# An order of its own for scores and DFT pairs in each of three stages, and a one-element ScalarE copy in each burst

## The chip, the cores and the metric

The kernel runs on one core of one Trainium2 chip, as one launch. The metric is the device time of that launch in microseconds. TensorE (PE) multiplies matrices; VectorE (DVE), ScalarE (ACT) and GpSimd (POOL) do the elementwise work; SyncE (SP) issues most DMAs. PEld is PE's weight load, which a trace lists apart from the matmul.

## The reference

Two branches read the same 2048 x 640 input, and a sigmoid gate mixes them.

```python
def _A_ref(x, wqkv, wo):                      # H = 32 heads, Dh = 20
    qkv = (x @ wqkv).reshape(B, S, 3, H, Dh).transpose(2, 0, 3, 1, 4)
    q, k, v = qkv[0], qkv[1], qkv[2]
    scores = jnp.einsum("bhqd,bhkd->bhqk", q, k) * (Dh ** -0.5)
    p = softmax(scores)
    o = jnp.einsum("bhqk,bhkd->bhqd", p, v)
    return o.transpose(0, 2, 1, 3).reshape(B, S, D) @ wo
def _B_ref(x, dft_seq_re, dft_seq_im, dft_hid_re, dft_hid_im):
    a = jnp.einsum("bsd,ed->bse", x, dft_hid_re)
    b = jnp.einsum("bsd,ed->bse", x, dft_hid_im)
    return jnp.einsum("ts,bse->bte", dft_seq_re, a) - jnp.einsum("ts,bse->bte", dft_seq_im, b)
g = sigmoid((x * gate_w).sum(-1, keepdims=True))
return g * _A_ref(x, wqkv, wo) + (1 - g) * _B_ref(x, ...)
```

The second branch is two matrix products with DFT matrices: along the 640 features ("hidden"), then along the 2048 positions ("sequence"). All is float32; where the kernel wants one pass of the array it splits a value into a rounded part and a rest and adds three products.

## The kernel before, in words

A first part (L543 to L632) projects q, k and v, stores them to DRAM and prepares the weights of the second branch. Then comes the main loop (L1117 to L1124), 256 **cycles**. In each cycle attention and the second branch are woven together, and PE's instructions are issued in exactly the order of a string of letters.

Attention is cut into 32 units: a pair of heads and one half of the queries. A head has 20 features, so a head's product needs under 64 rows of the array; of each pair one head lies on rows 0 to 63 and the other on rows 64 to 127. These are the two **halves** of the array, and a matmul on one half can run beside one on the other. The letters are:

- **e** (L1060 to L1091): one score matmul, 62 rows by 512 columns, into a PSUM bank (L1081), and ScalarE's exp of it into the tile p (L1087). Two e, one on each half, make one step `i`; a cycle has eight e, four steps. The first e of a step calls `begin(i)`, which sets `now[0] = i`, runs what was put off to that step (`at_step`), and takes a p tile, of which there are five.
- **m** (`s_mm`, L184 to L196): one score matmul for the row maxima of a unit 43 steps ahead (LEAD), into a PSUM bank (L194), and VectorE's max over it (L196). A cycle has eight m. When a unit's maxima are complete, `max_nm` and `turn_max` (L208, L226) turn them into two rows that later scores take in as extra rows.
- **F** (`fill`, L1005): as many steps of the second branch as the plan `goals` gives to this place. A step is a **DFT pair**: two matmuls of 64 rows by 320 columns, one on each half, into the PSUM tiles yp0 and yp1.
- **B** (`burst`, L1095): first up to two or three waiting `extras` (reading out yp, adding results), then the 8 products p times v of two key tiles (`av_step`, L720; each shows as two matmul records), which use all rows of the array. At the end of a unit, every eighth burst, ScalarE evicts av into o (L733).

Scores of both kinds take their banks from one ring of five (`bank`, L142). A score may start when the reader of the score five places earlier is done.

The string is `ORDER` for nearly all cycles, and `LATE` from cycle 246, when no m are left. `FIRST` says, for each of the four steps of a cycle and for each kind, on which half the first of the two scores goes.

The second branch runs through three stages in the cycles. **Hidden** (cycles 0 to 55, 15 pairs a cycle): `hid_pair`, L489 to L533, matmul at L511, read out by ScalarE and VectorE at L520 and L521. **Sequence** (56 to 223, 16 pairs a cycle, three cycles to an output tile): `dft_step`, L784 to L832, matmul at L807, read out at L826 and L827. **Output** (224 on, 12 pairs a cycle): `out_tile`, L866 to L899, the output projection of tiles already normalised, matmul at L878, read out at L887 to L890. `goals` spreads a cycle's pairs evenly over the F of its string; ORDER has 15 F.

The read of a finished yp is put into `extras` with the due time `now[0]`, and follow-up work with `now[0] + 3` or the like; `run_extras` in a burst takes what is due.

Of the kernel before, what the change touches and what calls it, by code (L numbers as in the profile page):

```python
# [22 lines left out]
DH = 20  # L23
# [9 lines left out]

ORDER = "emFemFFFFemFeFFmeFFemFFFmmFFmeeB"
LATE = "eeeeFFFFFFeeeEB"
FIRST = {"e": (0, 0, 1, 1), "m": (1, 1, 1, 1)}


LEAD = 43
# [49 lines left out]
def mix_kernel(ctx: ExitStack, tc: tile.TileContext, xa, xh, wqk, wb, wr, cdft, wo, out):  # L91
# [83 lines left out]

    mx, nms, ends = {}, {}, []
    rows_, done_tiles = [], []
    now, later = [-1], {}

    def at_step(i, fn):  # L180
        later.setdefault(i, []).append(fn)
# [307 lines left out]
    def hid_pair(u):  # L489
        n, hf, k = u // 8, u // 4 % 2, u % 4  # L490
        _, _, factor, targets = FEATURE[n]
        ps = [new_y(z)[:, :HE] for z in range(2)]
        fresh = [(th, ri, hf, k) not in seen for _, th, ri in targets]
        seen.update((th, ri, hf, k) for _, th, ri in targets)
        rows = [a_scr[ri, hf, th, k] for _, th, ri in targets]
        olds = []
        for (_, th, ri), new, row in zip(targets, fresh, rows):
            old = None
            if th == ri:
                old = acc(ri, hf, k)  # L500
            elif not new:
                old = slots.pop(0)
                slots.append(old)
                at_step(now[0] + 4, functools.partial(sp.dma_start, old, row))
            olds.append(old)
        done_ = 0
        for d in range(ND):
            for a, b in ((0, 0), (0, 1), (1, 0)):
                for z in range(2):
                    r = slice(64 * z, 64 * z + 64)  # L510
                    pe.matmul(ps[z], lefts[n][a][r, d, k * P : k * P + P], rights[2 * n + hf][r, b, d],  # L511
                              start=done_ == 0, stop=done_ == 3 * ND - 1)
                done_ += 1
                if done_ < 3 * ND:
                    yield
        direct = [i for i, ((_, th, ri), new) in enumerate(zip(targets, fresh)) if new and th == ri]
        m = olds[direct[0]] if direct else raw_tile()[:, : 2 * HE].rearrange("p (s c) -> p s c", s=2)

        def read():
            act.activation(m[:, 0], ps[0], AF.Copy, scale=factor)  # L520
            dve.tensor_scalar(m[:, 1], ps[1], factor, 1.0, op0=ALU.mult, op1=ALU.mult)  # L521

        def add(sign, old):
            pool.tensor_tensor(old, old, m, op=ALU.add if sign > 0 else ALU.subtract)  # L524

        extras.append((now[0], read))
        ends_ = {(th, ri): i for i, f in enumerate(FEATURE) for _, th, ri in f[3]}
        for (sign, th, ri), new, row, old in zip(targets, fresh, rows, olds):
            if not new:
                extras.append((now[0] + 3, functools.partial(add, sign, old)))  # L530
            if th != ri or ends_[th, ri] == n:
                at_step(now[0] + (4 if new else 11), functools.partial(sp.dma_start, row, m if new else old))
        yield  # L533

    step = 0
# [248 lines left out]
    def dft_step(g):  # L784
        n, t, s = g // NS // HT, g // NS % HT, g % NS
        if s == 0:
            new_y(0), new_y(1)
            outs[n, t] = []
        if s % 8 == 0 and g // 8 + 3 < 2 * UNITS:
            cfin.append(load_c(g // 8 + 3))  # L790
        if s % 8 == 4 and cfin and 2 < g // 8 + 2 < 2 * UNITS:
            cfin.pop(0)()
        if s == 8:
            for _, th, hf in PRODUCTS[n][2]:
                tt = th * HT + t
                y = None
                if (tt, hf) in signs:
                    y = apool[0].tile([P, HE], F32, name="yt", bufs=4)
                    sp.dma_start(y, y_scr[tt, :, hf * HE : (hf + 1) * HE])
                outs[n, t].append(y)  # L800
        c = cparts[g // 8]
        cs = slice((s % 8) * P, (s % 8 + 1) * P)
        a = at[n % 2, s]
        for z, (cz, az) in enumerate(((0, 0), (0, 1), (1, 0))):
            for h in range(2):
                r = slice(64 * h, 64 * h + 64)
                pe.matmul(yp[h][:, :HE], c[r, cz, cs], a[r, az], start=s == 0 and z == 0, stop=s == NS - 1 and z == 2)  # L807
            if z < 2:
                yield
        w = g % (HT * NS) - 16  # L810
        if n + 1 == len(PRODUCTS) and w >= 0:
            d, r = divmod(w, 8)
            if r == 0 and d < ND:
                wos[d] = raw_tile()[:, :D]
                sp.dma_start(wos[d], wo[:, d])
            if r == 5 and d < ND:
                raw = wos.pop(d)
                for h in range(2):
                    wos[d, h] = a_tile(1, 2 * d + h)
                    split(wos[d, h][:, 0], wos[d, h][:, 1], raw[:, h * HE : (h + 1) * HE], pool, pool)  # L820
        if s == NS - 1:
            m = apool[0].tile([P, HE], F32, name="m", bufs=3)
            y0, y1 = yp[0][:, :HE], yp[1][:, :HE]

            def read():
                act.activation(m, y0, AF.Copy)  # L826
                dve.tensor_tensor(m, y1, m, op=ALU.add)  # L827

            extras.append((now[0], read))
            for out_, y in zip(PRODUCTS[n][2], outs.pop((n, t))):  # L830
                extras.append((now[0] + 5, functools.partial(finish_y, out_, t, m, y)))
        yield  # L832


# [31 lines left out]
    def out_tile(tt, hf):  # L866
        new_y(0), new_y(1)
        if hf == 0:
            k = tt - PRE[0]
            yo[tt] = f32(a_tile(1, 12 + k) if k < 4 else a_tile(0, k)).rearrange("p z c -> p (z c)")  # L870
            assert all(st[tt, h] == 0 for h in range(2))
            sp.dma_start(yo[tt], y_scr[tt])
        o = opre[tt]
        for d in range(ND - 1):
            for z, (oz, wz) in enumerate(((0, 0), (0, 1), (1, 0))):
                for h in range(2):
                    r = slice(64 * h, 64 * h + 64)
                    pe.matmul(yp[h][:, :HE], o[r, oz, d], wos[d, hf][r, wz], start=d == 0 and z == 0, stop=d == ND - 2 and z == 2)  # L878
                if (d, z) != (ND - 2, 2):
                    yield  # L880
        m = apool[0].tile([P, HE], F32, name="m", bufs=3)
        y0, y1 = yp[0][:, :HE], yp[1][:, :HE]
        g = gate[:, tt : tt + 1]

        def read():
            if now[0] < total - LEAD:
                act.activation(m, y0, AF.Copy, scale=g)  # L887
            else:
                dve.tensor_scalar(m, y0, g, 1.0, op0=ALU.mult, op1=ALU.mult)
            dve.scalar_tensor_tensor(m, y1, g, m, op0=ALU.mult, op1=ALU.add)  # L890

        def add():
            y = yo[tt][:, hf * HE : (hf + 1) * HE]
            pool.tensor_scalar(y, y, ngate[:, tt : tt + 1], float(signs[tt, hf]), op0=ALU.mult, op1=ALU.mult)
            pool.tensor_tensor(y, y, m, op=ALU.add)  # L895

        extras.append((now[0], read))
        extras.append((now[0] + 3, add))
        yield  # L899

    def finish_y(target, t, m, y):
# [84 lines left out]
        at_tile += n  # L986
    assert cycles[-1][1] <= last + 1
    late = -(-(total - LEAD) // 4)
    at_goal = 0
    for c0, c1, count in cycles:  # L990
        for c in range(c0, c1):
            share = count * (c + 1 - c0) // (c1 - c0) - count * (c - c0) // (c1 - c0)
            places = (LATE if c >= late else ORDER).count("F")
            goals[c] = [at_goal + share * (f + 1) // places for f in range(places)]
            at_goal += share

# [58 lines left out]

    heads = {"e": 0, "m": 2 * LEAD}

    held = []

    def score(kind):  # L1060
        hold, kind = kind == "E", kind.lower()
# [1 line left out]
        heads[kind] += 1  # L1063
        i, z = divmod(x, 2)
        h = z
        if kind == "m" or i <= 4 * late:
            h ^= FIRST[kind][(i - (LEAD if kind == "m" else 0) - 1) % 4]
        if kind == "m":
            s_mm(i, h)()
            if z:  # L1070
# [4 lines left out]
        if i < total:  # L1075
# [8 lines left out]
            def exp():  # L1084
                if z == 0 and hold:
                    begin(i)
                act.activation(pts[n, kt, qc][:, h], pt, AF.Exp, scale=float(DH) ** -0.5)  # L1087
                if z:
                    end(i)

# [4 lines left out]
    def burst(c):  # L1095
# [8 lines left out]
                held.pop(0)()  # L1104
        turned[:] = ends
        ends.clear()
        if c == HID - 1:
            start_dft()

# [5 lines left out]
        else:  # L1115
            score(kind)
    for c in range(total // 4):  # L1117
        for kind in "e" * (c == late) + (LATE if c >= late else ORDER):
            if kind == "F":
                fill(c)  # L1120
            elif kind == "B":
                burst(c)
            else:
                score(kind)  # L1124
# [125 lines left out]
```

## Time and profile before

| what | value |
|---|---|
| median of 3 runs | 1848.58 us (1848.13 to 1849.0) |
| the profiled execution | 1848.44 us |
| its span, first to last instruction | 1846.7 us |
| mean granted TensorE clock | 1.000 |
| ACT, busy share of the span | 67% |
| POOL, busy share of the span | 71% |
| DVE, busy share of the span | 79% |
| DMA, mean | 189 GB/s |

PE is shown as busy for nearly the whole span, but its matmuls are pipelined, their ends are modelled, and two of them can run side by side. So busy time says little here. What can be read is when each matmul starts: the distance between two starts on the same half is what the first of them cost. The burst is a good mark in every cycle, since L726 occurs nowhere else; the distance from one burst's first matmul to the next is the length of a cycle. For DVE and ACT the number in brackets is the idle time ahead of a group and what ended it.

### The profile page before, as it was taken

The numbers are of one execution on the slowest core, as the hardware profiler recorded it, in microseconds if no ns is written. First come the engines' busy times: TensorE is split into PE (matmuls) and PEld (weight loads), VectorE is DVE, ScalarE is ACT, GpSimd is POOL, SyncE is SP. The second block draws the span as 40 slices with busy tenths as digits, with TensorE's granted clock in tenths as the row PEclk, the third lists the DMA queues.
The fourth block names the chain that finished last, engine by engine and source line by source line (L and its number), as shares of the span: only waits on it lengthen the run. The fifth ranks groups of instructions, "written<-read, shape, count | busy, mean of one in ns | idle before, by whom it ended". The sixth has DMA issues, their size and how long they took to land. (4 is left out here: it accounts for less than half of the span.)

```text
span 1846.7 us, 45912 instructions
## 1 busy us (share of the span) xinstructions
PE 1838.3 (100%) x17917; PEld 1339.6 (73%) x17917; DVE 1460.3 (79%) x2428; ACT 1237.2 (67%) x2378; POOL 1302.8 (71%) x1102
## 2 busy tenths in 40 slices
PE   9999999999999999999999999999999999999998
PEld 8988977676776776776777777677677777766666
DVE  4157489888888888888888888888888888889953
ACT  4233377777777777776676677677667767777785
POOL 1379735666678987556889899866889998724444
PEclk9999999999999999999999999999999999999999
DMA  7899884777666675536577687646486856442224
GB/s 237 191 316 357 310 219 133 225 222 236 205 218 212 197 218 146 142 108 171 182 221 240 162 252 192 198 127 182 148 224 186 233 165 204 137 115 65 64 56 156
DMA packets 196014, 349.63 MB, mean 189 GB/s; under 512 B 54240, under 2 KB 107616, under 8 KB 194004
## 3 DMA queue, kind: packets, MB, share of 16 engines
q1 hardware_dynamic: 194515, 341.45, 61.6%
q0 software_dynamic: 1280, 5.25, 1.4%
q8 instruction: 141, 2.31, 0.5%
q14 instruction: 78, 0.63, 0.1%
HBM read 257.79 MB, written 88.65 MB: 188 GB/s over the span
## 5 line engine op out<-in xcount | busy, mean ns | idle before, releaser
L196 DVE TENSOR_REDUCE mx<-ps 128x1 f32<-128x512 f32 x2048 | 1300.4, 686 | 205.4 <-PE ps L194 188.3
L1087 ACT ACTIVATE p<-ps 128x512 f32<-128x512 f32 x2048 | 1088.2, 598 | 421.6 <-PE ps L194 221.9
L194 PE MATMUL ps<-kst,qst 60*128 60x512 f32 x2048 | 777.0, 413 | 0.6 <-ACT p L372 0.5
L1081 PE MATMUL ps<-qst,kst 62*128 62x512 f32 x2048 | 694.5, 414 | 0.0
L807 PE MATMUL yp<-x,part 64*128 64x320 f32 x5376 | 644.9, 306 | 0.0
L807 PEld LDWEIGHTS yp<-x,part 64*128 64x128 f32 x5376 | 582.9, 186 | 7.2
L1081 PEld LDWEIGHTS ps<-qst,kst 62*128 62x128 f32 x2048 | 332.1, 184 | 222.8 <-DVE mx L196 129.8
L726 PE MATMUL av<-p,v 128*21 128x512 f32 x4096 | 492.5, 596 | 0.0
L194 PEld LDWEIGHTS ps<-kst,qst 60*128 60x128 f32 x2048 | 367.5, 184 | 12.4 <-ACT p L1087 1.0
L133 POOL TENSOR_TENSOR part<-raw,part 128x1024 fp32r<-128x1024 f32 (+3 forms) x134 | 297.0, 2216 | 10.2
L726 PEld LDWEIGHTS av<-p,v 128*21 128x21 f32 x4096 | 95.3, 100 | 207.1 <-issue 206.1
L132 POOL CAST part<-raw 128x1024 fp32r<-128x1024 f32 (+2 forms) x127 | 125.2, 986 | 134.2 <-PE yp L807 100.8
L672 POOL TENSOR_TENSOR raw<-raw,raw 128x1024 f32<-128x1024 f32 x78 | 187.3, 2401 | 34.0 <-DMA raw<-in_cdft 22.3
L511 PE MATMUL yp<-wb,x 64*128 64x320 f32 x1680 | 206.9, 307 | 0.0
L511 PEld LDWEIGHTS yp<-wb,x 64*128 64x128 f32 x1680 | 179.4, 186 | 3.3 <-DVE x L521 0.2
L524 POOL TENSOR_TENSOR x<-x,raw 128x640 f32<-128x640 f32 x40 | 62.6, 1564 | 44.1 <-DVE raw L521 40.6
L133 POOL TENSOR_TENSOR x<-araw,x 128x320 fp32r<-128x320 f32 x96 | 84.0, 875 | 7.7
L878 PE MATMUL yp<-x,part 64*128 64x320 f32 x720 | 87.1, 308 | 0.0
L895 POOL TENSOR_TENSOR x<-x,m 128x320 f32<-128x320 f32 x30 | 26.2, 874 | 79.2 <-DVE m L890 73.2
L878 PEld LDWEIGHTS yp<-x,part 64*128 64x128 f32 x720 | 75.9, 185 | 2.7
L701 POOL TENSOR_TENSOR araw<-araw 128x320 f32<-128x320 f32 x80 | 70.0, 876 | 3.2 <-DMA araw<-a_scr 1.4
L905 POOL TENSOR_TENSOR yt<-yt,m 128x320 f32<-128x320 f32 x64 | 55.4, 877 | 10.2 <-DVE m L827 10.2
(110 smaller groups left out, 1375.0 us busy)
## 6 DMA issues: line engine op xcount, KB each, us to landing
raw<-in_cdft SPq DMA_DIRECT2D x188, 512.0 KB
araw<-a_scr SPq DMA_DIRECT2D x176, 160.0 KB
qk_scr<-p SPq DMA_DIRECT2D x40, 512.0 KB
w_scr<-wb SPq DMA_DIRECT2D x36, 400.0 KB
kst<-qk_scr SPq DMA_DIRECT2D x90, 160.0 KB
qst<-qk_scr SPq DMA_DIRECT2D x90, 160.0 KB
wb<-w_scr SPq DMA_DIRECT2D x8, 1600.0 KB
part<-in_xh SPq DMA_DIRECT2D x10, 1024.0 KB
```

What stands on the lines that cost most here:

```text
L132: e1.tensor_copy(dst1, src)
L133: e2.tensor_tensor(dst2, src, f32(dst1), op=ALU.subtract)
L194: pe.matmul(ps, q[b : b + KROWS, qt * P : (qt + 1) * P], k[b : b + KROWS, kc * 512 : (kc + 1) * 512], start=True, stop=True)
L196: return lambda: dve.tensor_reduce(mx[n][:, h, qt, kc : kc + 1], ps, axis=AX.X, op=ALU.max)
L511: pe.matmul(ps[z], lefts[n][a][r, d, k * P : k * P + P], rights[2 * n + hf][r, b, d], start=done_ == 0, stop=done_ == 3 * ND - 1)
L672: pool.tensor_tensor(raws[0], raws[0], raws[1], op=ALU.add if PRODUCTS[n][0][1][0] > 0 else ALU.subtract)
L701: pool.tensor_tensor(raws[0], raws[0], raws[1], op=ALU.add if PRODUCTS[n][1][1][0] > 0 else ALU.subtract)
L726: pe.matmul(av[32 * j : 32 * j + DH + 1, :], v[:, kt, h * (DH + 1) : (h + 1) * (DH + 1)], pp[qc][:, h, :], start=kt == 0, stop=kt == NS - 1)
L807: pe.matmul(yp[h][:, :HE], c[r, cz, cs], a[r, az], start=s == 0 and z == 0, stop=s == NS - 1 and z == 2)
L878: pe.matmul(yp[h][:, :HE], o[r, oz, d], wos[d, hf][r, wz], start=d == 0 and z == 0, stop=d == ND - 2 and z == 2)
L1081: pe.matmul(pt, k[b : b + KROWS + 2, kt * P : (kt + 1) * P], q[b : b + KROWS + 2, qc * 512 : (qc + 1) * 512], start=True, stop=True)
L1087: act.activation(pts[n, kt, qc][:, h], pt, AF.Exp, scale=float(DH) ** -0.5)
```

## The change

The one string becomes four plans, each a string with its own FIRST. The plan is chosen by the cycle. The pair of numbers at the places of `e` and `m` is the half of a step's first score.

```diff
-ORDER = "emFemFFFFemFeFFmeFFemFFFmmFFmeeB"
-LATE = "eeeeFFFFFFeeeEB"
-FIRST = {"e": (0, 0, 1, 1), "m": (1, 1, 1, 1)}
+HIDDEN = "emeFFmeFFFmeFFFmeFFmeFeFFFmFemmB", {"e": (0, 0, 1, 1), "m": (1, 1, 0, 1)}
+SEQUENCE = "emeFmFFFFemFeFFmeFFemFFFmmFFFmeeB", {"e": (0, 0, 1, 1), "m": (1, 1, 1, 1)}
+OUTPUT = "emFeFmFemeFFmeFFmeFFmFmFeFmeB", {"e": (1, 0, 0, 1), "m": (0, 1, 1, 0)}
+LATE = "eeeeFFFFFFeeeEB", {"e": (0, 0, 0, 0), "m": (0, 0, 0, 0)}
...
-    now, later = [-1], {}
+    now, at_cycle, later = [-1], [0], {}
+
+    def ended():
+        return min(now[0], 4 * at_cycle[0] + 3)
...
-        extras.append((now[0], read))
+        extras.append((ended(), read))
...
+    def plan(c):
+        return LATE if c >= late else OUTPUT if c >= edge[-1] else SEQUENCE if c >= HID else HIDDEN
+
...
-            places = (LATE if c >= late else ORDER).count("F")
+            places = plan(c)[0].count("F")
...
-        if kind == "m" or i <= 4 * late:
-            h ^= FIRST[kind][(i - (LEAD if kind == "m" else 0) - 1) % 4]
+        h ^= plan(at_cycle[0])[1][kind][(i - (LEAD if kind == "m" else 0) - 1) % 4]
...
-                act.activation(pts[n, kt, qc][:, h], pt, AF.Exp, scale=float(DH) ** -0.5)
+                newest[:] = [pts[n, kt, qc][:, h]]
+                act.activation(newest[0], pt, AF.Exp, scale=float(DH) ** -0.5)
...
         turned[:] = ends
         ends.clear()
+        if 4 * c + 4 < total:
+            act.activation(seen_, newest[0][0:1, 0:1], AF.Copy)
...
     for c in range(total // 4):
-        for kind in "e" * (c == late) + (LATE if c >= late else ORDER):
+        at_cycle[0] = c
+        for kind in "e" * (c == late) + plan(c)[0]:
```

Every `now[0]` in a due time of a read-out or of its follow-up (in `hid_pair`, `dft_step` and `out_tile`) becomes `ended()`, which never goes past the third step of the cycle. `seen_` is a tile of one element. The copy reads one element of the p tile half that the newest exp wrote, so ScalarE waits for that exp and then writes `seen_`.

The number of F is now 15 in HIDDEN, 16 in SEQUENCE and 12 in OUTPUT, one for each pair of the cycle. Every string still has eight e and eight m, four of each on either half.

More of the change, by code (lines that the diff above doesn't have):

```diff
@@ L529, in hid_pair @@
             if not new:
-                extras.append((now[0] + 3, functools.partial(add, sign, old)))
+                extras.append((ended() + 3, functools.partial(add, sign, old)))
             if th != ri or ends_[th, ri] == n:
-                at_step(now[0] + (4 if new else 11), functools.partial(sp.dma_start, row, m if new else old))
+                at_step(ended() + (4 if new else 11), functools.partial(sp.dma_start, row, m if new else old))
         yield
@@ L827, in read @@
                 dve.tensor_tensor(m, y1, m, op=ALU.add)
-            extras.append((now[0], read))
+            extras.append((ended(), read))
             for out_, y in zip(PRODUCTS[n][2], outs.pop((n, t))):
-                extras.append((now[0] + 5, functools.partial(finish_y, out_, t, m, y)))
+                extras.append((ended() + 5, functools.partial(finish_y, out_, t, m, y)))
         yield
@@ L895, in add @@
             pool.tensor_tensor(y, y, m, op=ALU.add)
-        extras.append((now[0], read))
-        extras.append((now[0] + 3, add))
+        extras.append((ended(), read))
+        extras.append((ended() + 3, add))
         yield
@@ L1056, in mix_kernel @@
     heads = {"e": 0, "m": 2 * LEAD}
-    held = []
+    held, newest = [], []
+    seen_ = const.tile([1, 1], F32, name="seen")
     def score(kind):
```

## The prediction

> **What bounds the kernel now.** I read the page first, then single cycles of the trace, engine by engine, then windows by stage.
>
> ```profile
> span 1846.7 us, 45912 instructions
> ```
>
> The profiled execution took 1848.44 us, so 1.74 us lie around this span; the median of the runs, 1848.58, is 0.14 above it. To get at the stages I asked for the busy time of the max reductions (L196) in three windows that begin and end at bursts. Columns: window, its length, DVE busy time and count, clock, DMA.
>
> ```profile
> 240.99:578.98 337.99, 274.55 (x433) 1.00 0.68 205
> 585.39:1640.76 1055.37, 848.99 (x1337) 1.00 0.63 182
> 1647.34:1763.32 115.98, 94.47 (x152) 1.00 0.28 79
> ```
>
> A cycle has eight reductions, so these are 54, 167 and 19 cycles: 6.26 us a cycle in the hidden stage, 6.32 in the sequence stage, 6.10 in the output stage. The clock is full throughout. They hold 1509 of the 1847 us; nothing outside the cycles is touched. Now one sequence cycle, PE alone (start, length, group):
>
> ```profile
> 1002.33 0.63 PE L726 MATMUL av<-p,v 128*21 128x512 f32 x4
> ...
> 1004.66 0.39 PE L194 MATMUL ps<-kst,qst 60*128 60x512 f32 x1
> ...
> 1004.89 0.75 PE L807 MATMUL yp<-x,part 64*128 64x320 f32 x8
> ...
> 1008.26 0.42 PE L1081 MATMUL ps<-qst,kst 62*128 62x512 f32 x2
> 1008.62 1.91 PE L726 MATMUL av<-p,v 128*21 128x512 f32 x16
> 1010.46 0.49 PE L1081 MATMUL ps<-qst,kst 62*128 62x512 f32 x1
> ```
>
> From burst to burst 6.29; the burst holds PE from 1008.62 to 1010.46, 1.84 us. Between, each half of the array has its own stream. A score takes 0.235 us of its half (1004.66 to 1004.89), a fill 0.147 (eight fills are four a half: 0.75 less the 0.31 of the last, over three). A half has eight scores and 16 fills: 8 x 0.235 + 16 x 0.147 = 4.23. About 0.10 is lost when scores follow the burst, and 0.12 from the end of the last score to the burst (1008.26 to 1008.62 less 0.235). The sum is 4.23 + 0.22 + 1.84 = 6.29, what was measured. **The sequence stage is bound by the array itself**, with nothing left between. By the same sum the hidden stage (15 fills) should take 6.15 and the output stage (12) 5.71; they take 0.11 and 0.39 more. What ends last there:
>
> ```profile
> 403.89 0.63 PE L726 MATMUL av<-p,v 128*21 128x512 f32 x4
> 405.73 0.50 PE L1081 MATMUL ps<-qst,kst 62*128 62x512 f32 x1
> 406.31 5.15 DVE L196 TENSOR_REDUCE mx<-ps 128x1 f32<-128x512 f32 x8 [0.70 <-PE ps L194]
> 408.97 2.48 DVE L196 TENSOR_REDUCE mx<-ps 128x1 f32<-128x512 f32 x4
> 409.52 0.39 PE L194 MATMUL ps<-kst,qst 60*128 60x512 f32 x1
> 409.75 0.46 PE L1081 MATMUL ps<-qst,kst 62*128 62x512 f32 x2
> 410.14 1.05 PE L726 MATMUL av<-p,v 128*21 128x512 f32 x7
> ```
>
> Scores share five PSUM banks in turn, so a score waits for the reader of the score five places before it. In the old order e8 stands five behind m5. The fifth reduction starts at 408.97 (four are left from there), takes 0.69, ends at 409.66, and the two last e start at 409.75. **PE stood still for a bank.** The output stage shows the same more strongly:
>
> ```profile
> 1001.71 1.88 DVE L196 TENSOR_REDUCE mx<-ps 128x1 f32<-128x512 f32 x3
> 1702.29 0.63 PE L726 MATMUL av<-p,v 128*21 128x512 f32 x4
> 1704.71 5.00 DVE L196 TENSOR_REDUCE mx<-ps 128x1 f32<-128x512 f32 x8 [0.28 <-PE ps L194]
> 1707.91 0.55 PE L1081 MATMUL ps<-qst,kst 62*128 62x512 f32 x2
> 1708.40 1.92 PE L726 MATMUL av<-p,v 128*21 128x512 f32 x16
> 1709.98 0.55 DVE L890 SCALAR_TENSOR_TENSOR m<-yp,gate,m 128x320 f32<-128x320 f32 x1 [0.27 <-ACT m L887]
> ```
>
> Reductions back to back step by 0.60 (the row of three: 1.88 less 0.68, over two). Here the chain is a loop: burst, first m, five reductions on DVE, bank free, e8, burst. DVE idles only 0.28 and 0.27 in 6.1 us.
>
> **The change part by part.**
>
> *Order of the hidden stage.* The scores now stand e1 m1 e2 m2 e3 m3 e4 m4 e5 m5 e6 e7 m6 e8 m7 m8. e8 stands behind e5, and m5's bank is wanted by m7, with a score, four fills and another score (0.235 + 4 x 0.147 + 0.235 = 1.06) or more between on its half. I set the start of every score by its half's sum and asked for each bank's reader: m1's reduction begins 0.58 after the first score (405.73 to 406.31), the next ones 0.60 apart or 0.47 after their score. An exp begins 0.59 after the first score, or 0.47 after its own, takes 0.60, and PE starts some 0.1 after its end (as 409.66 to 409.75). The tightest are m3, at 0.10 + 2 x 0.235 + 5 x 0.147 = 1.31 on its half, with e1's exp over at 0.59 + 0.60 and the bank free at 1.29, and m8 (3.95, e6's bank free at 3.9). m7 wants m5's bank at 3.95; that reduction ends at 3.05 + 0.69, so it is free at 3.8. So none stops PE, barely, and the floor is 6.15. Both halves still carry 8 scores and 15 fills. The last reduction and the read of yp (L521) move later, to about 2.0 us after the burst's start; the first fill on the second half then stands at 2.4, so that is hidden too. Gain at most 0.11 a cycle, at least 0. I take 0.085, because two banks come free with hardly 0.05 to spare: 55 cycles x 0.085 = **4.7 us** (0 to 6.1).
>
> *Order of the output stage.* Scores: e1 m1 e2 m2 e3 m3 e4 m4 e5 m5 e6 m6 m7 e7 m8 e8. Now m8 stands five behind m5, and it is issued together with e8, so the loop stays. What goes is the gap in the five reductions (eight took 5.00; 7 x 0.60 + 0.69 is 4.89) and part of the wait for e8: m5 done at 1704.71 + 4 x 0.60 + 0.69 = 1707.80, pair at 1707.85, burst 0.39 to 0.43 later, at 1708.24 to 1708.28 against 1708.40. I take 0.10 for 21 cycles (the 22nd has no m left): **2.1 us** (0 to 3.4). DVE's wait for L887 goes as well, since ACT has one exp after the burst's start instead of two, but DVE then waits longer for m1: worth nothing.
>
> *Order of the sequence stage.* The old string has 15 fill places for 16 pairs, and the last place took two; the new one has 16. Beyond this only e2 moves ahead of the first fill. The halves' sums stay, m1's wait and the end stay: **0**. The bounds: 6.32 less 6.29 over 167 cycles, 5 us, is all that could go; nothing shows that it would.
>
> *The copy.* A ScalarE instruction of one element stands last in each burst, behind the exps, the read of yp and, where a head pair's unit ends, the eviction of av (L733).
>
> ```profile
> 89.14 0.16 ACT L396 ACTIVATE logit<-ps 128x1 f32<-128x1 f32 x1
> 89.18 0.45 ACT L392 ACTIVATE v<-ps 128x320 f32<-128x320 f32 x1
> 629.50 0.63 PE L726 MATMUL av<-p,v 128*21 128x512 f32 x4
> 631.53 0.60 ACT L733 ACTIVATE o<-av 128x512 f32<-128x512 f32 x1 [0.84 <-issue]
> 632.02 1.08 ACT L1087 ACTIVATE p<-ps 128x512 f32<-128x512 f32 x2
> 635.88 1.92 PE L726 MATMUL av<-p,v 128*21 128x512 f32 x16
> 1004.76 3.24 ACT L1087 ACTIVATE p<-ps 128x512 f32<-128x512 f32 x6 [1.24 <-PE ps L194]
> L1087 ACTq EVENT_SEMAPHORE  x403: 17/17/17, 587.8 to 1639.3; - x135
> ```
>
> In an ordinary cycle ACT waits 1.24 us ahead of its first exp: the copy lies in that gap and costs nothing, and its wait for the newest exp ends inside it too. Where a unit ends (every eighth burst) there is no gap: L733 cannot start before av is done, and e1's exp comes 0.49 behind it, 2.52 after the burst's start instead of 2.43 (1004.76 less 1002.33). That 0.09 already shows in full: this cycle takes 6.38. Behind the copy wait e1's exp, then m3 for its bank. The copy's price there has as ends 0.04 (89.14 to 89.18, the step from an activation of one column to the next) and about 0.28 (0.16 to 0.18 of its own and 0.10 of lost overlap). It may also save: the exps that reuse a p tile carry a semaphore instruction of 17 ns, which the copy may make needless, so the low end is -0.02. I take 0.05, nearest to the small activation's own row: 30 unit ends in these three stages x 0.05 = **+1.5 us** (-0.6 to +8.4).
>
> *The cap on due times* (ended): with e7 ahead of the last fills, now would be one step further; the cap puts due times where they were. 0.
>
> Sum: -4.7 - 2.1 + 0 + 1.5 = -5.3 on 1848.44, and 0.14 for the median: **1843.3 us**.
>
> **The rivals.**
>
> *A. The array keeps start order (slower).* The new orders put scores of one half in a row, so a half must run ahead. The trace shows how far it does so now:
>
> ```profile
> 1005.47 0.39 PE L1081 MATMUL ps<-qst,kst 62*128 62x512 f32 x1
> 1005.48 0.44 PE L194 MATMUL ps<-kst,qst 60*128 60x512 f32 x1
> 1005.71 0.45 PE L807 MATMUL yp<-x,part 64*128 64x320 f32 x3
> 1005.90 0.39 PE L1081 MATMUL ps<-qst,kst 62*128 62x512 f32 x1
> ```
>
> The program has one pair of fills between this m and the next e, but three fills start first: the third overtook an e that waited for its half. The old order needs one matmul overtaken, the new hidden and output orders two at one place each. If starts kept program order, a pair behind a score on the first half would leave the other idle: following the strings at 0.235 and 0.147 gives 0.65 more a hidden cycle, 0.09 a sequence cycle, 0.79 an output cycle, 36 + 15 + 17 = 68 us: 1917. It decides from the point where a second matmul has to be passed. The row of three speaks against it. The Trainium skill, TensorE: Matmul & The Clock Gate, "Part 3: Packing small matmuls — row/col tiling", says "MATMULs are pc-monotone in start AND end — strict FIFO, no reordering"; by that rule rival A holds, and the rows above disagree with it. Chance 0.08, and 0.03 for being slower in another way.
>
> *B. The gain does not come (within 0.2%).* Passing one matmul but not two costs 0.088 a hidden cycle (0.235 less 0.147), just what the bank gave: 1848. Or m3 and m8 find their banks late by some hundredths. Or the copy costs 0.28 at unit ends: 30 x 0.28 = 8.4, which with the 6.8 gained gives 1850.2. Together 0.33.
>
> *C. The copy removes no wait.* Should the exps keep the semaphore instruction of the row above, nothing changes in the sum: I have given it no gain. That case lies inside the forecast.
>
> **How the numbers follow.** Forecast 0.56, with both stages between half and all of their gain: 1838.5 to 1844.8. B 0.33, A and the rest 0.11. A measurement of this kernel tells about 0.2%, 3.7 us, from no change; so faster 0.56, same 0.33, slower 0.11. The range reaches from the full floors (-6.1 - 3.4 - 0.6 = -10.1) to B's upper end: 1838.5 to 1850.2.
>
> **What would show it.** Hidden cycles near 6.17 with the last two m less than 0.1 behind the fills; output cycles near 6.00 with eight reductions in about 4.9 us; sequence cycles at 6.29 still. Unit ends: the copy between L733 and e1's exp, and that cycle some 0.05 longer than 6.38. I am wrong if hidden cycles stay at 6.25 (banks or run-ahead), if sequence cycles move at all (then the array was not their bound), or if ACT's gap ahead of the first exp is gone in ordinary cycles.

## The result, and the profile after

| | before | changed |
|---|---|---|
| median of 4 runs each | 1848.37 us (1848.13 to 1849.0) | 1839.17 us (1838.49 to 1839.51) |
| profiled execution | 1848.44 us | 1838.49 us |
| ratio of the times | | 0.9948, 95% interval 0.9935 to 0.9961 |

The changed kernel is 9.2 us faster, 0.4 to 0.65%. In its code the lines have moved: a score e is L1089, its exp L1096, a score m L198, its max L200, the fills L515, L811 and L882, the burst's products L730, the eviction of av L737, and the copy is L1117.

The page of the changed kernel begins with its span; before it was 1846.7.

```profile
span 1836.7 us, 45512 instructions
```

It has 400 instructions fewer (45912 before), although a copy was added to 255 of the 256 cycles. That is the first thing to be explained. Next, the busy time of the max reductions in windows between the same bursts as before the change (columns: window, length, DVE busy and count, clock, DMA share, GB/s).

```profile
239.98:575.08 335.10, 274.40 (x433) 1.00 0.68 208
581.49:1632.72 1051.23, 846.09 (x1338) 1.00 0.62 183
1638.89:1753.32 114.43, 92.84 (x153) 1.00 0.29 80
```

The 54 hidden cycles fell from 337.99 to 335.10 us, the 167 of the sequence stage from 1055.37 to 1051.23, the 19 of the output stage from 115.98 to 114.43. Two of the prediction's windows end a little before the burst that they were to end at (at 578.98 and 1640.76, where the bursts start at 579.06 and 1641.03), so the whole cycles of before are 338.07 and 1055.64. **The largest gain, 4.4 us, lies in the sequence stage, for which the prediction had 0.** The rest of the difference in span, 10.0 less 8.9, is mostly the first burst, which starts 1.2 us earlier; it starts at 233.3 to 235.4 in the kernels below, whatever was edited, so nothing is read from it.

One hidden cycle, PE alone:

```profile
388.99 1.92 PE L730 MATMUL av<-p,v 128*21 128x512 f32 x16
390.84 0.50 PE L1089 MATMUL ps<-qst,kst 62*128 62x512 f32 x1
...
393.59 0.52 PE L1089 MATMUL ps<-qst,kst 62*128 62x512 f32 x2
...
394.56 0.40 PE L1089 MATMUL ps<-qst,kst 62*128 62x512 f32 x1
394.63 0.31 PE L515 MATMUL yp<-wb,x 64*128 64x320 f32 x1
394.78 0.40 PE L198 MATMUL ps<-kst,qst 60*128 60x512 f32 x2
395.11 0.63 PE L730 MATMUL av<-p,v 128*21 128x512 f32 x4
```

From burst to burst 6.12. The last e starts among the fills and no longer waits for m5's reduction; the last two m follow the last fill, and the burst follows them at 0.33. The floor in the prediction was 6.15. An output cycle, PE and then DVE:

```profile
1687.13 1.91 PE L730 MATMUL av<-p,v 128*21 128x512 f32 x16
...
1692.78 0.39 PE L198 MATMUL ps<-kst,qst 60*128 60x512 f32 x1
1692.78 0.39 PE L1089 MATMUL ps<-qst,kst 62*128 62x512 f32 x1
1693.10 0.63 PE L730 MATMUL av<-p,v 128*21 128x512 f32 x4
```

```profile
1688.43 0.55 DVE L894 SCALAR_TENSOR_TENSOR m<-yp,gate,m 128x320 f32<-128x320 f32 x1
1689.54 4.88 DVE L200 TENSOR_REDUCE mx<-ps 128x1 f32<-128x512 f32 x8 [0.56 <-PE ps L198]
```

5.97, with m8 and e8 side by side at the end, eight reductions in 4.88 (5.00 before), and DVE's wait moved from the read-out, which has none now, to the first m (0.56 instead of 0.28). All four points are those of the prediction. Now a sequence cycle, PE and then ACT:

```profile
996.85 1.92 PE L730 MATMUL av<-p,v 128*21 128x512 f32 x16
...
1000.01 0.39 PE L198 MATMUL ps<-kst,qst 60*128 60x512 f32 x1
...
1003.12 0.63 PE L730 MATMUL av<-p,v 128*21 128x512 f32 x4
```

```profile
998.08 0.20 ACT L1117 ACTIVATE seen<-p 1x1 f32<-1x1 f32 x1
999.23 3.27 ACT L1096 ACTIVATE p<-ps 128x512 f32<-128x512 f32 x6 [0.95 <-PE ps L198]
```

6.27 instead of 6.29. The copy lies in ACT's gap, as forecast. But two things differ from before. e1's exp starts 2.38 after the burst's start, not 2.43. And the third m (at 1000.01) takes 0.39, where the old one, at 1005.48 in the prediction's rows, took 0.44: it had found its bank late. What the copy takes away is counted in the view of the exp's own line, first before, then after (columns: durations in ns, first and last start; ACTq is ScalarE's sequencer):

```profile
L1087 ACTq EVENT_SEMAPHORE  x662: 17/17/38, 229.4 to 1818.7; - x166
```

```profile
L1096 ACTq EVENT_SEMAPHORE  x6: 17/17/254, 228.3 to 1770.3; - x6
```

656 semaphore instructions are gone and 255 copies came: 401 fewer, the 400 of the page but for one. (The new orders alone leave 613 of the 662, as x1_no_copy shows below; the copy alone leaves 6.) By the trace's records of sequence cycles before the change, e1's exp and the fifth exp of a cycle always, and the third in 43% of them, waited for two semaphores, PE's and ScalarE's own (an earlier exp had written the same p tile). Since the copy waits for the newest exp, later exps need only PE's.

### The profile page after: what moved, and what is told of

It is laid out like the page before. It is cut to its first block, busy times and chain, and to the rows that moved or that the text cites. A ratio compares the mean times of both kernels' runs of the same rounds, so it can differ in the third digit from the quotient of the medians.

```text
span 1836.7 us, 45512 instructions
## 1 busy us (share of the span) xinstructions
PE 1828.5 (100%) x17917; PEld 1327.4 (72%) x17917; DVE 1455.6 (79%) x2428; ACT 1261.9 (69%) x2633; POOL 1303.9 (71%) x1102
## 5 line engine op out<-in xcount | busy, mean ns | idle before, releaser
L200 DVE TENSOR_REDUCE mx<-ps 128x1 f32<-128x512 f32 x2048 | 1295.3, 685 | 208.0 <-PE ps L198 159.1
L1096 ACT ACTIVATE p<-ps 128x512 f32<-128x512 f32 x2048 | 1080.9, 599 | 379.8 <-PE ps L1089 195.5
L198 PE MATMUL ps<-kst,qst 60*128 60x512 f32 x2048 | 768.2, 409 | 1.2 <-DMA a_scr<-x 0.7
L1089 PE MATMUL ps<-qst,kst 62*128 62x512 f32 x2048 | 680.6, 406 | 0.0
L811 PE MATMUL yp<-x,part 64*128 64x320 f32 x5376 | 651.5, 306 | 0.0
L811 PEld LDWEIGHTS yp<-x,part 64*128 64x128 f32 x5376 | 590.0, 186 | 6.6
L730 PE MATMUL av<-p,v 128*21 128x512 f32 x4096 | 492.5, 596 | 0.0
L1089 PEld LDWEIGHTS ps<-qst,kst 62*128 62x128 f32 x2048 | 328.4, 184 | 221.8 <-DVE mx L200 123.9
L198 PEld LDWEIGHTS ps<-kst,qst 60*128 60x128 f32 x2048 | 360.6, 184 | 15.8 <-ACT p L1096 1.6
L730 PEld LDWEIGHTS av<-p,v 128*21 128x21 f32 x4096 | 95.3, 100 | 208.3 <-issue 207.0
L515 PE MATMUL yp<-wb,x 64*128 64x320 f32 x1680 | 212.5, 307 | 0.6 <-DVE x L525 0.6
L515 PEld LDWEIGHTS yp<-wb,x 64*128 64x128 f32 x1680 | 193.8, 186 | 5.0 <-DVE x L525 1.6
L882 PE MATMUL yp<-x,part 64*128 64x320 f32 x720 | 92.9, 311 | 0.0
L882 PEld LDWEIGHTS yp<-x,part 64*128 64x128 f32 x720 | 80.7, 186 | 1.8
```

Source lines behind the costliest of these rows:

```text
L198: pe.matmul(ps, q[b : b + KROWS, qt * P : (qt + 1) * P], k[b : b + KROWS, kc * 512 : (kc + 1) * 512], start=True, stop=True)
L200: return lambda: dve.tensor_reduce(mx[n][:, h, qt, kc : kc + 1], ps, axis=AX.X, op=ALU.max)
L730: pe.matmul(av[32 * j : 32 * j + DH + 1, :], v[:, kt, h * (DH + 1) : (h + 1) * (DH + 1)], pp[qc][:, h, :], start=kt == 0, stop=kt == NS - 1)
L1089: pe.matmul(pt, k[b : b + KROWS + 2, kt * P : (kt + 1) * P], q[b : b + KROWS + 2, qc * 512 : (qc + 1) * 512], start=True, stop=True)
L1096: act.activation(newest[0], pt, AF.Exp, scale=float(DH) ** -0.5)
```

## The experiments

Each kernel ran beside the kernel before the change, on the same chip. Cycle lengths are the median distance between the first matmuls of two bursts, in the profiled execution: ordinary cycles of each stage; hidden cycles whose burst holds `max_nm` (every eighth); sequence cycles whose burst ends a unit (every eighth). Over all sequence cycles that end no unit, the medians come out up to 0.01 higher. All in us.

| kernel | hidden | with max_nm | sequence | unit end | output |
|---|---|---|---|---|---|
| before | 6.24 | 6.25 | 6.288 | 6.38 | 6.10 |
| the change | 6.12 | 6.29 | 6.266 | 6.445 | 5.99 |
| x1_no_copy | 6.12 | 6.31 | 6.30 | 6.38 | 6.01 |
| x2_copy_alone | 6.20 | 6.21 | 6.265 | 6.44 | 6.06 |
| x13_copy_other | 6.12 | 6.32 | 6.285 | 6.46 | 6.00 |
| x3_sequence_alone | 6.24 | 6.24 | 6.293 | 6.37 | 6.085 |
| x5_hidden_alone | 6.12 | 6.30 | 6.30 | 6.37 | 6.085 |
| x6_output_alone | 6.24 | 6.24 | 6.30 | 6.38 | 6.01 |
| x4_copy_first | 6.12 | 6.28 | 6.266 | 6.38 | 5.99 |
| x10_unlevel | 6.24 | 6.325 | 6.266 | 6.45 | 5.99 |
| x8_gate_and_loads | 6.12 | 6.31 | 6.266 | 6.38 | 5.995 |
| x9_read_before_max | 6.125 | 6.17 | 6.266 | 6.37 | 5.99 |
| x11_ngate_on_pool | 6.13 | 6.17 | 6.266 | 6.38 | 5.99 |

**1. Orders or copy.** The change without the copy, the copy alone in the kernel before, and the change with a copy that reads another tile.

```diff
 # x1_no_copy, against the change
-        if 4 * c + 4 < total:
-            act.activation(seen_, newest[0][0:1, 0:1], AF.Copy)
 # x2_copy_alone, against the kernel before
+    held, newest = [], []
+    seen_ = const.tile([1, 1], F32, name="seen")
...
+                newest[:] = [pts[n, kt, qc][:, h]]
+                act.activation(newest[0], pt, AF.Exp, scale=float(DH) ** -0.5)
...
+        if 4 * c + 4 < total:
+            act.activation(seen_, newest[0][0:1, 0:1], AF.Copy)
 # x13_copy_other, against the change
+    still_ = const.tile([1, 1], F32, name="still")
+    dve.memset(still_, 0.0)
...
-            act.activation(seen_, newest[0][0:1, 0:1], AF.Copy)
+            act.activation(seen_, still_, AF.Copy)
```

> The change without the copy. My theory: the copy lets e1's exp start some 60 ns sooner in an ordinary cycle (0.53 instead of 0.59 us after the first score), and m3, which waits for e1's bank, is what the sequence cycle gains by. Then without it ordinary sequence cycles go back to about 6.29 us, unit-end cycles there go from 6.44 to about 6.38, and the time is about 1841 us (+3 and some tenths in the hidden stage, -1.4 and -0.6 at unit ends). Rival: moving e2 ahead of the first fill is the gain, and the copy only costs. Then ordinary sequence cycles stay at 6.265 and the time falls to about 1837 us.

> The kernel before with nothing but the copy. My theory: ordinary sequence cycles 6.265 instead of 6.29 (126 x 0.025 = -3 us), unit-end cycles there 6.44 instead of 6.38 (21 x 0.06 = +1.3), hidden and output stages unchanged since their bank waits are on VectorE: about 1846.7 us. Rival (the copy only costs): sequence cycles at 6.29, and 1849.5 to 1850 us.

> The changed kernel, with the copy of one element at the same place, but out of a tile of its own that is written once at the start, and not out of the newest p. It costs ScalarE the same and takes over no wait. Theory: the copy gains because it reads what the newest exp wrote, so that the next exp need not wait on its own engine's semaphore; without that, e1's exp begins 0.59 us after its score again (0.534 with the change), sequence cycles take 6.30 (6.265 with it), unit ends are still some 0.06 longer than with no copy, and the time is that of the change without the copy or a little more, 1844 to 1847. Rival: it gains because ScalarE has done something shortly before (any instruction would serve); then e1's exp begins at 0.53 to 0.54, sequence cycles take 6.265, and the time is near 1839 to 1840.

Measured: x1_no_copy 1845.31 (1842.57 to 1848.88), ratio 0.9979 [0.997, 0.9987]; x2_copy_alone 1843.58 (1842.06 to 1845.45), 0.9967 [0.9954, 0.998], both beside a before of 1849.01; x13_copy_other 1847.05 (1844.88 to 1848.73), 0.9984 [0.9975, 0.9993], beside 1849.22. So by the medians the three orders together gave 3.7 us and the copy alone 5.4: **more than half of the gain is the copy's**. The two add up to about the change (9.2, and 8.2 in part 6). x13_copy_other came out between its two theories: the time, 1847.05, is that of a copy that takes over no wait, e1's exp starts 0.534 after its score, as in the change, and the sequence cycle, 6.285, lies between. The lines of the exps show why, of x1_no_copy and of x13_copy_other:

```profile
L1096 ACTq EVENT_SEMAPHORE  x613: 17/17/38, 228.7 to 1817.3; - x154
```

```profile
L1098 ACTq EVENT_SEMAPHORE  x416: 17/17/38, 228.6 to 1818.6; - x139
```

By the records, this copy too waits for ScalarE's own semaphore, since it writes `seen_` again, and that wait is old enough to cover e1's exp and no more: of 147 sequence cycles that end no unit e1's exp has a second semaphore in none, the fifth exp still in all, the third in 63. With 613, 416 and 6 such instructions the sequence cycle is 6.30, 6.285 and 6.266. The own part of the wait is what counts, and a copy serves as far as its own wait reaches. Had any recent ScalarE instruction served, the fifth exp, with exps just ahead of it, would not have been late. It starts, after e1's score, at 2.754, 2.726 and 2.705 in the three kernels (medians). The third m, whose bank e1's exp frees, needs only e1's part: the next fill on its half follows it by 0.276, 0.238 and 0.232. What one wait costs is the step of e1's exp: 0.593 to 0.534, some 0.06 us, though the semaphore instruction is shown with 0.017.

**2. Each order alone**, without the copy: one new string, the old string in the other two stages.

```diff
 # x5_hidden_alone, against the change without the copy
-SEQUENCE = "emeFmFFFFemFeFFmeFFemFFFmmFFFmeeB", ...
-OUTPUT = "emFeFmFemeFFmeFFmeFFmFmFeFmeB", ...
+SEQUENCE = "emFemFFFFemFeFFmeFFemFFFmmFFmeeB", ...
+OUTPUT = "emFemFFFFemFeFFmeFFemFFFmmFFmeeB", ...
```

> The sequence stage's order alone, with no copy. My theory: sequence cycles at 6.29, time 1848.4 us as before. Rival (e2's move is the gain): sequence cycles at 6.265, time about 1844.5 us.

> The hidden stage's order alone, without the copy. My theory: ordinary hidden cycles fall from 6.24 to 6.12 us, but the order also brings three losses of its own: the gate's five small instructions (make_gate, due at step 40) now stand ahead of the cycle's last three reductions and cost cycle 10 about 1 us; after a unit's last maxima the read of yp ends too late for the next cycle's first fill, 6.30 instead of 6.25 in one cycle of eight; and the first reductions of unit 8 wait for a late load in cycle 53, 0 to 8 us from run to run. So about 41 x 0.12 = 4.9 gained, 1.0 + 0.4 + some 2 lost: 1847 us, between 1845 and 1851. Rival (the prediction's own working, nothing lost beside it): 1843.7 us.

> The kernel before with the OUTPUT order alone: no copy, the old order in the hidden and sequence stages. Theory: the loop through the five reductions and e8 gets 0.08 to 0.10 us shorter in each of 21 output cycles (6.09 to about 6.00), 1.7 to 2.1 us in all: near 1847 where before shows 1849. Rival: the output cycles gain only through the earlier first exp, which the copy gives; then they stay at 6.08 or more and the time is that of before within 0.5 us.

Measured: sequence alone 1847.86 (1847.31 to 1851.85), 0.9995 [0.9986, 1.0004] beside 1849.01; hidden alone 1845.66 (1844.25 to 1849.95), 0.9977 [0.9965, 0.9989] beside 1849.38; output alone 1847.28 (1845.83 to 1851.74), 0.9991 [0.9982, 1.0] beside 1849.22. The sequence order is worth nothing that can be measured. The output order takes some 0.08 from a cycle, and the sum of its 21 cycles goes from 128.39 to 126.87. The hidden order takes 0.12 from an ordinary cycle, more than the forecast's 0.085, and yet its 55 cycles sum to 340.89 instead of 344.29, 3.4 us and not 6.6. The table shows one leak: cycles whose burst holds `max_nm` are at 6.30. The other is a cycle of 7.5 us, the tenth. Both are followed up in part 5. Taken alone the three orders give 1.2 (within the noise), 3.7 and 1.9 us, 6.8 in all, and together (x1_no_copy) only 3.7. In the profiled executions cycle 53 is 4.0 too long in x1_no_copy and has no stall in x5_hidden_alone, which would account for the difference; it is not shown for the other executions.

**3. The copy's place.**

```diff
 # x4_copy_first, against the change
         run_extras(max(done - HIDS, 0) // 3, 3 if c <= HID else 2)
+        if 4 * c + 4 < total:
+            act.activation(seen_, newest[0][0:1, 0:1], AF.Copy)
         for kt in (2 * c, 2 * c + 1):
...
-        if 4 * c + 4 < total:
-            act.activation(seen_, newest[0][0:1, 0:1], AF.Copy)
```

> The change with the copy issued ahead of the burst's products, so that at a unit's end it stands before the eviction of av and not between that and e1's exp. My theory: the saving of the semaphore instruction stays in every cycle, and the cost at unit ends goes: e1's exp there at about 0.67 us after the first score instead of 0.77, unit-end sequence cycles at 6.36 instead of 6.44, hidden ones at 6.16 instead of 6.26; 21 x 0.08 + 7 x 0.1 = 2.4 less, about 1836.8 us. Rival (the eviction's own wait for av sets that cycle and the copy hides in it): no change, 1839.2 us.

Measured: 1838.23 (1836.49 to 1843.85), 0.9944 [0.9932, 0.9956] beside 1849.01. ScalarE at the end of a unit, in the change and in x4_copy_first:

```profile
1030.27 0.60 ACT L737 ACTIVATE o<-av 128x512 f32<-128x512 f32 x1 [0.51 <-POOL x L134]
1030.77 0.18 ACT L1117 ACTIVATE seen<-p 1x1 f32<-1x1 f32 x1
1030.86 3.15 ACT L1096 ACTIVATE p<-ps 128x512 f32<-128x512 f32 x6
```

```profile
1036.17 0.18 ACT L1109 ACTIVATE seen<-p 1x1 f32<-1x1 f32 x1
1036.81 0.60 ACT L737 ACTIVATE o<-av 128x512 f32<-128x512 f32 x1 [0.45 <-POOL x L133]
1037.30 3.17 ACT L1096 ACTIVATE p<-ps 128x512 f32<-128x512 f32 x6
```

In the change the exp starts 0.59 behind L737, in x4_copy_first 0.49: the copy puts 0.09 (1030.77 to 1030.86) into a chain without a gap. Moved ahead of the products it lies in a gap there too, the unit end falls from 6.445 to 6.38, and ordinary cycles keep 6.266.

**4. How far a half may run ahead.** All first m of a step on one half again, in the hidden stage: by the sum of its matmuls one half of the array would then run 0.47 ahead of the program's order, past three waiting matmuls.

```diff
-HIDDEN = "emeFFmeFFFmeFFFmeFFmeFeFFFmFemmB", {"e": (0, 0, 1, 1), "m": (1, 1, 0, 1)}
+HIDDEN = "emeFFmeFFFmeFFFmeFFmeFeFFFmFemmB", {"e": (0, 0, 1, 1), "m": (1, 1, 1, 1)}
```

> The change with the hidden stage's m on the halves that the other stages use, 1 1 1 1 instead of 1 1 0 1: the halves' sums stay equal, but from e5 to m6 one half must run 0.47 us ahead of the other instead of 0.235, passing three matmuls that wait instead of two. If PE takes any order across the halves: hidden cycles stay at 6.12 us, 1839 us. If a half can run ahead by no more than what the levelled order needs: 0.235 more a hidden cycle, 6.35 us, 13 us slower, 1852 us. By strict start order the levelled order itself could not have gained, so that is out already.

Measured: 1845.24 (1843.6 to 1847.83), 0.9972 [0.9961, 0.9984] beside 1849.38. Hidden cycles take 6.24 where the change takes 6.12. DVE and PE of x10_unlevel:

```profile
396.90 0.69 DVE L200 TENSOR_REDUCE mx<-ps 128x1 f32<-128x512 f32 x1
```

```profile
397.65 0.50 PE L1089 MATMUL ps<-qst,kst 62*128 62x512 f32 x1
...
397.99 0.45 PE L515 MATMUL yp<-wb,x 64*128 64x320 f32 x3
```

Behind this sixth e the next fill of its half starts 0.34 later, where 0.235 is the rule: 0.10 of the 0.12 are lost here. But the trace points to a bank, not to a limit on running ahead. The sixth e takes the bank of m3, the score five places before it, and m3's reduction is the DVE row above; it ends at 397.60. In 52 of 53 hidden cycles (all but the tenth) this e starts 0.054 to 0.057 behind the end of that reduction, early or late, and is shown with 0.49 to 0.50. In the change, where it stands behind m5 on its half, it starts 0.27 behind that end and is shown with 0.39. The e8 of the old output stage, which waited for its bank, has the same two figures, 0.054 and 0.50 (medians). The sixth e did overtake m5, which the program issues before it and which starts at 397.87. By this reading the new place of m5 brings the sixth e to a bank that is not yet free; no edit tests it. How many waiting matmuls a half can pass, no run here shows. That the halves are kept level is a part of the change that carries weight: 0.12 a cycle.

**5. The leaks of the hidden stage.** Three edits, one on top of the other, all with the copy placed first as in part 3. x8: `make_gate` moves from step 40 into the burst of the tenth cycle, behind the read-out, and two loads of rows that the hidden stage has written to a_scr (`load_a_early`) are issued one cycle later, clear of the loads of the next unit's scores. x9: the read-out goes ahead of `max_nm` in the burst. x11: the last product of the gate goes to POOL.

```diff
 # x8_gate_and_loads, against x4_copy_first
-    at_step(40, make_gate)
...
-                if c in (HID - 9, HID - 7, HID - 5):
-                    for s in {9: (8, 0), 7: (4,), 5: (12,)}[HID - c]:
+                if c in (HID - 9, HID - 6, HID - 4):
+                    for s in {9: (8, 0), 6: (4,), 4: (12,)}[HID - c]:
...
+        if c == 9:
+            make_gate()
 # x9_read_before_max, against x8_gate_and_loads
+        run_extras(max(done - HIDS, 0) // 3, 3 if c <= HID else 2)
         for n in ends:
             max_nm(n)
-        run_extras(max(done - HIDS, 0) // 3, 3 if c <= HID else 2)
 # x11_ngate_on_pool, against x9_read_before_max
-        dve.tensor_scalar(ngate, gate, -1.0, 1.0, op0=ALU.mult, op1=ALU.add)
+        pool.tensor_scalar(ngate, gate, -1.0, 1.0, op0=ALU.mult, op1=ALU.add)
```

> The change with the copy first in the burst, the gate's instructions put into the burst of cycle 9, behind the read of yp, and two early loads of the transformed rows moved one cycle later, so that they no longer hold up the DMA queue ahead of the loads of k and q. My theory: cycle 10 falls from 7.1 to about 6.15 us, the wait in cycle 53 goes or falls below 0.5 us, unit ends as in the run with the copy first: 1839.2 - 1.0 - 2.4 - 1.0 = about 1834.8 us. Rival (cycle 53 waits for the DMA engines, which are full there whatever the order of the queue): cycle 53 still at 7 us or more, 1836 us or above, and scattered by some us.

> The kernel of the run above, and in each burst the read of yp ahead of a unit's maximum (max_nm). My theory: in hidden cycles after a unit's last maxima the first fill no longer waits for the read, so they fall from 6.28 to about 6.18 us, sequence cycles stay: 7 x 0.1, that is 0.7 us less than the run above. Rival (the fill waits for ScalarE's half of the read, or for the maximum's own users): those cycles stay at 6.28 and the time is that of the run above.

> The version of the fifth experiment's follow-up (copy first, gate and loads moved, read ahead of the max), with one edit more: the small product that makes ngate (128x16, tensor_scalar) is issued on POOL and no longer on DVE. Theory: that instruction took 0.85 to 1.33 us on DVE only because it stood beside a tensor_tensor of POOL and ended 0.03 behind it; on POOL it stands in POOL's own queue and DVE goes on at once. Then the tenth cycle falls from about 7.2 us to 6.2 to 6.3, and the run is 0.9 to 1.1 us shorter, near 1834.0 on a before of 1849. Rival: the cycle is long for another reason (the exp of the gate on ScalarE ahead, or the reductions' order); then it stays at 7.1 to 7.2 and the time stays near 1835.

Measured: x8 1836.78 (1835.92 to 1838.95), 0.9925 [0.9904, 0.9946]; x9 1835.03 (1834.56 to 1838.74), 0.9918 [0.9893, 0.9942], both beside 1849.38; x11 1834.34 (1833.68 to 1835.1), 0.9919 [0.9905, 0.9932], beside 1849.22.

*max_nm.* DVE of the change at such a burst, then PE:

```profile
409.01 0.29 DVE L215 TENSOR_REDUCE nm<-mx 128x32 f32<-128x128 f32 x1
409.22 0.48 DVE L525 TENSOR_SCALAR raw<-yp 128x320 f32<-128x320 f32 x1
```

```profile
409.21 0.50 PE L1089 MATMUL ps<-qst,kst 62*128 62x512 f32 x1
...
409.56 0.76 PE L515 MATMUL yp<-wb,x 64*128 64x320 f32 x4
```

The read-out of yp ends at 409.70, after the first fills could start; four of them take 0.76, with a hole. With the read-out first, x9's DVE shows:

```profile
408.50 0.48 DVE L525 TENSOR_SCALAR raw<-yp 128x320 f32<-128x320 f32 x1
408.89 0.28 DVE L215 TENSOR_REDUCE nm<-mx 128x32 f32<-128x128 f32 x1
```

These cycles fall from 6.31 to 6.17, all seven of them.

*Cycle 10.* It takes 7.1 us in the change. My theory for x8 was that the gate's instructions stood in the wrong place on DVE. **It fell**: with them moved the cycle was still 1.1 too long. The group of one DVE instruction, before and after (busy us and mean ns behind the bar), says more:

```profile
L638 DVE TENSOR_SCALAR ngate<-gate 128x16 f32<-128x16 f32 x1 | 0.2, 175 | 0.0
```

```profile
L642 DVE TENSOR_SCALAR ngate<-gate 128x16 f32<-128x16 f32 x1 | 0.9, 853 | 0.0
```

The same work takes 0.175 or 0.853. In x9's timeline, of DVE and of POOL, it is 1.33:

```profile
291.51 1.33 DVE L642 TENSOR_SCALAR ngate<-gate 128x16 f32<-128x16 f32 x1
```

```profile
291.24 1.57 POOL L528 TENSOR_TENSOR x<-x,x 128x640 f32<-128x640 f32 x1 [1.26 <-issue]
```

It ends 0.03 behind the POOL instruction beside it (292.84 and 292.81), and in the change too (290.26 and 290.23). In the kernel before nothing of POOL ran beside it. The reductions and the read-out wait behind it. In x1_no_copy, x5_hidden_alone, x10_unlevel and x13_copy_other ngate takes 0.175, and yet their tenth cycle is 7.5: there another tensor_scalar of the gate (L640) stands beside the POOL instruction and takes 1.22 to 1.28, until 0.02 to 0.03 behind its end. On POOL, in x11, ngate is short again:

```profile
L642 POOL TENSOR_SCALAR ngate<-gate 128x16 f32<-128x16 f32 x1 | 0.2, 200 | 4.9 <-DVE gate L641 4.9
```

The tenth cycle then takes 6.13 (7.23 in x9), as expected. The medians, 1835.03 and 1834.34, are from different chips and their ranges touch; the 1.1 us of this cycle are shown by the trace alone.

*Cycle 53.* Its length varies from kernel to kernel: 1.0 too much in the profiled execution of the change, 4.0 in x13_copy_other, none in x5_hidden_alone. What waits there, from x13's waits (us in total, times, longest), and its windows (length, busy of PE, PEld, DVE, ACT, POOL, then the granted clock, DMA share and GB/s):

```profile
PE ps L198 <- DMA qst<-qk_scr: 2.1, 1, 2.1
```

```profile
558.88:560.68 1.80, 0.00 (x0) 0.00 (x0) 0.00 (x0) 0.58 (x1) 1.74 (x2) 1.00 0.64 237
...
561.58:564.48 2.90, 2.90 (x22) 2.90 (x20) 1.95 (x3) 1.61 (x3) 2.81 (x3) 0.50 0.92 269
565.08:567.08 2.00, 2.00 (x23) 1.45 (x23) 1.83 (x5) 1.95 (x4) 2.00 (x3) 1.00 0.87 303
```

The first m of a new unit waits for its rows of q, whose loads stand on SP behind the early loads of a_scr. PE stands still for 2.1 us, and then **the granted clock is 0.50** for some 3 us: a wait of 2.1 makes the cycle 4.0 longer. In x3_sequence_alone, in x1_no_copy and in x4_copy_first PE's rows at this place are:

```profile
564.16 0.46 PE L198 MATMUL ps<-kst,qst 60*128 60x512 f32 x1 [1.48 <-DMA qst<-qk_scr]
```

```profile
560.75 0.47 PE L198 MATMUL ps<-kst,qst 60*128 60x512 f32 x1 [2.18 <-DMA qst<-qk_scr]
```

```profile
563.16 0.76 PE L198 MATMUL ps<-kst,qst 60*128 60x512 f32 x1 [4.89 <-DMA qst<-qk_scr]
```

Their cycles are 1.9, 4.0 and 7.6 too long. After 1.48 the clock stays at 1.00; after 2.18 and 4.89 it falls to 0.50. With the loads one cycle later none of the three profiled runs (x8, x9, x11) has it. But four of the eleven with the loads in their old place have no such stall either (before, x5, x6, x10), so three are few to go by. All three show another, of 0.9 to 2.3 us in cycle 119, where a score e waits for its extra rows. In x8 that is

```profile
979.00 0.59 PE L1088 MATMUL ps<-qst,kst 62*128 62x512 f32 x2 [1.96 <-DMA qst<-m_scr]
```

and the clock stays at 1.00 behind it. In cycle 119 the unedited change is 0.5 too long in one run of two. The cause of this wait stays open.

**6. The change once more**, unedited, beside x6, x11 and x13.

> The changed kernel once more, unedited, on the chip of the runs beside it. Theory: sequence cycles 6.265, hidden 6.12, output 5.99, one stall of 0.9 to 1.4 us in cycle 10 and one of 0 to 7 us in cycle 53; near 1839 to 1840 where before shows 1849, ratio 0.994 to 0.996. Rival: the first measurement of it was a lucky one, and it comes out like the change without the copy, at 1843 or more.

Measured: 1841.0 (1840.7 to 1842.62), 0.9957 [0.9944, 0.9971] beside 1849.22. Hidden 6.12, sequence 6.266, output 5.99 as in the first profile; the stalls differ, 2.3 us in the hidden stage and 2.4 in the sequence stage, where the first profile has 2.4 and 0.3. x11 is 6.7 us ahead of it on the same chip. It has the lowest median of all; as a share of before, 0.9919, it is level with x9 (0.9918).

## Why the prediction was right, and where its steps were not

The time lay inside the forecast's own range, but two terms of the sum were off in opposite directions: the orders were to give 6.8 and gave 3.7 (x1), the copy was to cost 1.5 and gained 5.4 (x2). That the time fell inside 1838.5 to 1844.8 is in part luck: without the copy's gain, for which there was no term, it would have been 1845.3 (x1, beside a before of 1849.0).

- *Hidden order, -4.7:* the mechanism is right, the size per ordinary cycle was too small (0.12, not 0.085), and the step that failed is "the first fill on the second half then stands at 2.4, so that is hidden too". In seven cycles `max_nm` stands ahead of the read, 0.15 each; and no term was there for the single cycles 10 and 53. Alone it gave 3.4 in the profiled execution.
- *Output order, -2.1:* right; 1.5 alone (x6), 1.8 with the copy, by the chain that was named, at the cycle that was named, 6.00.
- *Sequence order, 0:* right (x3). But the reading behind it, "The sequence stage is bound by the array itself, with nothing left between", was too strong. For the hidden order m3's bank was reckoned free at 1.29 against 1.31, with exp starting at 0.59; m3 stands just as far behind the burst in the old sequence order (two scores and five fills), and there the row of 0.44 at 1005.48 shows it late. Single starts of the trace of before say by how much: its next fill comes 0.27 behind it (median), not 0.235.
- *The copy:* the step that failed is "the copy lies in that gap and costs nothing", followed by "I have given it no gain". It did cost nothing there. But the semaphore instruction of 17 ns, quoted in the prediction, was priced by its own length and only at unit ends. It stands for a wait of 0.06 ahead of an exp for which a bank is wanted, in every cycle. The prediction named the sign to look for, that it would be wrong "if sequence cycles move at all". At unit ends the price was right in kind: 0.065 and not 0.05, on 21 sequence cycles, with about 0.07 on the rest; x4 gives it back.
- *Rival A*, the array keeping start order, asked for 0.65 more a hidden cycle; it took 0.12 less. Whether there is a limit further on is open: the loss in x10 is read as a wait for a bank.
- *Rival B:* none of its three forms came. *Rival C* is refuted by the count of 662 and 6.

## What to carry to other kernels

Where an engine waits for a semaphore of its own in addition to another's, price the wait by what it does to the start (here 0.06 us), not by the length of the semaphore instruction; one tiny instruction that takes over the wait, placed in a gap of that engine, may remove it from all that follow. After a reordering, look at the single long cycles, not only at the ordinary one: here two of them took back 2.0 us in the change's own profile and 8.6 in that of x4_copy_first, where a halved clock followed the wait. And when a banked ring seems to come out even within some hundredths, read the start of the very next instruction before calling the array the bound.

## What the runs showed of the hardware that I had not expected

- A DVE tensor_scalar of 128x16 from SBUF to SBUF took 0.85 to 1.33 us instead of 0.175, until 0.03 after the POOL tensor_tensor beside it ended. The Trainium skill, SBUF — State Buffer, "Who interferes with whom", says that a tensor_scalar can enter a mode in which it needs the port pair that it shares with GpSimd, and that whoever comes first keeps the pair for the whole instruction. The three rows agree, and x11 with them.
- A stall of 2.1 us is enough to halve PE's granted clock for some 3 us (x13, windows above; 2.18 in x1 as well), while 1.48 us (x3) and 1.96 us (x8) left it at 1.00. The Trainium skill, TensorE: Matmul & The Clock Gate, "Part 1: The HAM clock gate (the "warmup" mystery)", puts the fall behind an idle window of about 3.4 us. The stall of 4.89 agrees; the two shorter ones do not, and here the measurement decides.
- Matmuls of one half of the array start ahead of earlier ones of the other half: in x10 the sixth e, at 397.65, ahead of m5, at 397.87, which stands before it in the program. No run here shows a limit to this.
